# Three of four rounds convolved along the free dimension by VectorE and GpSimd, the fourth by TensorE

## The chip, the cores and the metric

The kernel runs on one core of a Trainium2 chip. The core has TensorE (matrix products into PSUM), VectorE, ScalarE, GpSimd and SyncE; each runs its own instruction stream in order, and they wait for each other through semaphores. DMA transfers are issued from the queues of SyncE, ScalarE and GpSimd. The metric is the device time of one execution in microseconds (us). A profile of one execution gives, for every instruction, its start, its duration and what it waited for. In profiles PE is TensorE's matmul, PEld its weight load, DVE is VectorE, ACT ScalarE, POOL GpSimd and SP SyncE; L381 is line 381 of the kernel.

## The reference, cut to what matters

```python
# x: (8, 3904, 192) float32, weight: (8 heads, 7 taps)
w = softmax(weight, axis=-1)
x_pad = zeros of 6 tokens ahead of each of the 8 sequences, then x
for each head h (24 channels) and token s:
    conv[b, s, h, :] = sum over k of w[h, k] * x_pad[b, s + k, h, :]
y = conv.reshape(31232, 192)
a = y @ w1; b = y @ w2            # 192 x 1024 each
out = ((a * b) @ w3) @ w_out      # 1024 x 1024, 1024 x 192
```

The convolution is causal: a token's value is a weighted sum of that token and the six before it, with one set of seven weights for each head, and it does not look across the start of a sequence.

## The kernel before, in words

The 31232 tokens are two streams of 15616 tokens (`NS = 2`, `TS`), four sequences each, worked side by side: stream 0 lives in partitions 0 to 63 of a tile and stream 1 in partitions 64 to 127. A *round* is 512 tokens of both streams (`CH`), so there are 31 rounds, the last of half size. Rounds are taken in *groups* of four (`GROUP`); a group first does all its first products and then all its second products.

*First product* (`first_product`, `first_factor` at L381): for each of eight column blocks of 128, TensorE multiplies the transposed tokens `xT` by w1 and by w2, each into a pair of PSUM banks; ScalarE casts the first pair to bf16 (`asb`, L389) and VectorE multiplies it by the second pair into `abT` (L400). *Second product* (`second_product`, L434): w3 and w_out are multiplied once at the start into `W_sb`, so that a round and stream needs only `abT` times `W_sb`: 32 matmuls into one pair of banks, copied by ScalarE to an `osb` buffer (L439) and sent out by one DMA. There are five `osb` buffers (the tag `slot`), and a copy waits until the DMA that read its buffer before is done. `W_sb`'s source `w3T` is a constant tile of the kernel before.

PSUM is four pairs of banks. `banks()` takes the first pair of the list `free`, and `drained(p)` puts a pair back at its end. The list is a matter of the program's text and not of time: which pair an instruction gets is fixed when the program is written, and the instruction then waits for the pair's earlier reader.

*Convolution*: x is loaded by GpSimd's DMA queue in windows of 64 tokens that advance by 58 (`load_x`, L119): partition = token in the window, so the seven taps reach across partitions. `conv` (L290) multiplies a window by a 64x64 band matrix that holds a head's seven weights on its diagonals; VectorE or ScalarE moves the result from PSUM to `convo` (L311). `store` writes `convo` to `rows`, a token-by-token copy in DRAM, by SyncE's queue (L334), and `transposes` reads `rows` back into `xT` by DMA transposes (L363), three for a round. `xT` is a ring of four rounds. Blocks of windows are listed in `SIZES`: six small ones in the prologue, then six of 36 windows, one per group, whose heads are convolved after the second, fourth and eighth second product of a group for the group after next. `send` issues the transposes of a round as soon as its rows are stored. The order on each engine is the order of the program's text (`manual_schedule`); nothing reorders it later.

SyncE's queue issues its DMAs in the order of the text as well: the outputs of the second products, the stores of `rows` and the transposes stand in one line, and one that waits holds those behind it. The output DMAs of group 0 go by GpSimd's queue.

Of the kernel before, what the change touches and what calls it, by code (L numbers as in the profile page):

```python
# [8 lines left out]
FP32 = mybir.dt.float32  # L9
BF16 = mybir.dt.bfloat16  # L10
# [6 lines left out]
def kernel(  # L17
# [31 lines left out]
    SIZES = [6, 4, 8, 10, 8, 20] + [36] * 6  # L49
    assert sum(SIZES) == NWIN  # L50
    NB = len(SIZES)
    FIRST = [sum(SIZES[:b]) for b in range(NB)]
    PROLOGUE_BLOCKS = 6
    EARLY = SIZES[0] * ST
    MAXN = max(SIZES) // 2

# [203 lines left out]

    xT = [const.tile([128, RING + Q], BF16, name=f"xT{k}", tag=f"xT{k}") for k in range(NP)]
# [12 lines left out]
    def conv(b, h0, nh, evict=None):  # L274
        n = SIZES[b] // 2
        if h0 == 0:
            convo_of[b] = work.tile([128, n, NP, NS, Q], BF16, tag="convo", bufs=2, name="convo")
# [132 lines left out]
    def first_product(R, between=None, fts=range(JT), behind_conv=False):  # L410
        if R not in abT_of:
            first_tile(R)
        N = width(R)
        step = CH // N
        for ft in fts[::step]:
            first_part(R, list(range(ft, ft + step)), 0, N)
            if behind_conv and ft == step:
                free[1], free[2] = free[2], free[1]
            if between and ft in between:
                between[ft]()  # L420
# [34 lines left out]
    w3T = const.tile([128, JT, DFF], BF16)  # L455
# [105 lines left out]
    load_x(6)  # L561
    first_product(3)
# [5 lines left out]
    def conv_heads(b, heads, last, f=(nc.vector.tensor_copy,), nh=1):  # L568
        for j, h in enumerate(heads[::nh]):
            conv(b, h, nh, (f[j % len(f)],))  # L570
        if heads[-1] == H - 1:
            first = min(need(sent[0]), FIRST[b] + SIZES[b])
            store(b, last=first)
            send(last)
            store(b, first)
            send(last)

    slots = (range(0, 3), range(3, 6), range(6, H))
    zero(5)
    for jt in range(JT):  # L580
        w3_product(jt)

    groups = [list(range(R, min(R + GROUP, NR))) for R in range(0, NR, GROUP)]
    assert groups[-1][-1] == NR - 1
    for p, rounds in enumerate(groups):
        b = PROLOGUE_BLOCKS + p
        order = rounds[-1:] + rounds[:-1] if rounds[-1] == NR - 1 else rounds
        for j, R in enumerate(order if p else ()):
            first_product(R, behind_conv=j == 0 and b <= NB)
            send(R + GROUP)  # L590
            if j < 2 and b < NB:
                P(out=pace, in_=abT_of[R][0:1, JT - 1, 1, 0:2])  # L592
                load_x(b, (j,))
        if b < NB:
            zero(b)
        ahead = rounds[-1] + GROUP
        at = {1: [(b, slots[0], ahead)], 3: [(b, slots[1], ahead)],
              7: [(b, slots[2], ahead, (V, A))]}
        if p == 0:
            at = {0: [(5, range(0, 6), ahead, (V, A), 2)], 1: [(5, range(6, H), ahead, (V,), 2)],  # L600
                  4: at[1], 5: at[3], 7: at[7]}
        for i, (R, r) in enumerate((R, r) for R in rounds for r in range(NS)):
            second_product(R, r, R == NR - 1 and r == 1, nc.sync if p else nc.gpsimd)
            for c in at.get(i, ()) if b < NB else ():
                conv_heads(*c)
    assert sent[0] == NR
# [30 lines left out]
```

## Time and profile before

| what | value |
|---|---|
| time, median of 3 runs | 519.98 us (519.84 to 521.27) |
| profiled execution | 520.47 us, span 518.8 us, granted TensorE clock 1.0 |
| TensorE matmul busy | 512.4 us, 99% of the span |
| VectorE / ScalarE / GpSimd busy | 352.8 / 328.7 / 58.5 us |
| a group's first products (219.04 to 260.59) | 41.55 us |
| a group's second products (195.77 to 219.04) | 23.27 us |

The span is the time from the first to the last instruction of the profiled execution. Busy time is the union of an engine's instructions. The chain of waits follows the last instruction back to what released it, step by step; the share of an engine or a line in it says how much of the span that line itself set. A row of the groups gives the source line, the engine, the operation, the tiles it writes and reads, their sizes and the number of instructions, then busy time and mean duration, then how long the engine had been idle before them and for whom it waited.

### The profile page before, as it was taken

The page shows a single profiled execution, that of the slowest core. Times are in us where ns is not written, and L with a number is a line of the kernel's source. Part 1 is how long each engine was busy: PE and PEld are TensorE (multiplying, and loading weights), DVE is VectorE, ACT ScalarE, POOL GpSimd, SP SyncE. Part 2 cuts the span into 40 slices and gives each one's busy share as a digit, 9 for nine tenths or more (in the row PEclk, how much of TensorE's full clock was granted, in tenths as well). Part 3 has the DMA queues.
Part 4 walks back from the last instruction along what each step waited for, and adds up shares of the span by engine and source line. Part 5 has one row for each costly group of instructions (what it writes and reads, how often), then busy time and mean ns, then how long its engine had stood idle before and what let it go on. Part 6 is the DMA issues. An engine that isn't in the chain of part 4 may idle for free.

```text
span 518.8 us, 13029 instructions
## 1 busy us (share of the span) xinstructions
PE 512.4 (99%) x5576; PEld 338.7 (65%) x5576; DVE 352.8 (68%) x334; ACT 328.7 (63%) x415; POOL 58.5 (11%) x98
## 2 busy tenths in 40 slices
PE   8999999999999999999999999999999999999997
PEld 4455797445884558845588455884558845599567
DVE  6778625999439994399943999439994399921980
ACT  6887634777347773477734777347773477734762
POOL 8501522110001200011000120001200000000000
PEclk9999999999999999999999999999999999999999
DMA  9979997599246992469924699246992465124004
GB/s 117 162 145 133 156 201 202 137 178 119 93 134 134 151 121 92 135 117 142 143 92 136 141 141 122 93 136 147 133 121 93 136 146 96 37 92 153 1 3 152
DMA packets 133576, 64.61 MB, mean 125 GB/s; under 512 B 90460, under 2 KB 132798, under 8 KB 133454
## 3 DMA queue, kind: packets, MB, share of 16 engines
q1 hardware_dynamic: 94476, 44.06, 41.7%
q0 software_dynamic: 38896, 19.62, 29.1%
q8 instruction: 43, 0.70, 0.6%
q14 instruction: 15, 0.12, 0.1%
q10 hardware_dynamic: 146, 0.10, 0.1%
HBM read 33.25 MB, written 36.52 MB: 134 GB/s over the span
## 4 chain that ended last, share of the span: by engine, by line
PE 95%; DMA 2%; ACT 2%; DVE 1%; issue 0%; ACTq 0%; DVEq 0%
PE pairs L381 58%; PE pairs L434 31%; PE pairs L290 3%; DMA xT<-rows 2%; DVE abT L400 1%; PE pairs L469 1%; ACT asb L389 1%; PE pairs L206 1%; PE pairs L343 1%; PE pairs L256 0%; ACT wd L186 0%; ACT convo L311 0%; DVE convo L478 0%; ACT xT L355 0%; PE pairs L509 0%
## 5 line engine op out<-in xcount | busy, mean ns | idle before, releaser
L400 DVE TENSOR_TENSOR abT<-asb,pairs 128x1024 bf16<-128x1024 bf16 (+1 forms) x245 | 297.9, 1217 | 52.6 <-ACT asb L389 36.6
L381 PE MATMUL pairs<-xT,wd 64*128 64x512 bf16 (+3 forms) x3000 | 319.9, 371 | 1.1 <-DMA xT<-rows 0.5
L389 ACT CAST asb<-pairs 128x1024 bf16<-128x1024 f32 (+1 forms) x245 | 247.2, 1009 | 66.2 <-PE pairs L381 65.9
L381 PEld LDWEIGHTS <-wd 64*128 64x128 bf16 x3000 | 161.0, 94 | 154.8 <-issue 3.7
L434 PEld LDWEIGHTS <-abT 128*128 128x128 bf16 x1952 | 160.0, 98 | 7.5 <-issue 7.5
L434 PE MATMUL pairs<-W_sb,abT 128*128 128x192 bf16 x1952 | 164.9, 246 | 0.0
L439 ACT COPY osb<-pairs 128x384 f32<-128x384 f32 x122 | 58.3, 478 | 113.8 <-PE pairs L434 113.8
L311 DVE CAST convo<-pairs 128x864 bf16<-128x864 f32 (+5 forms) x58 | 46.4, 854 | 95.8 <-PE pairs L290 74.9
L119 POOL DMA_DIRECT2D xb<-in_x_dram x42 | 32.2, 784 | 3.7 <-PE pairs L381 3.7
L592 POOL COPY pace<-abT 1x2 bf16<-1x2 bf16 x10 | 1.8, 176 | 253.5 <-DVE abT L400 253.5
L290 PE MATMUL pairs<-xb,Aband 64*64 64x432 bf16 (+5 forms) x384 | 16.7, 284 | 0.1
L311 ACT CAST convo<-pairs 128x864 bf16<-128x864 f32 (+4 forms) x20 | 11.8, 626 | 0.4
L290 PEld LDWEIGHTS <-Aband 64*64 64x64 bf16 x384 | 6.9, 106 | 6.8 <-issue 5.7
L446 POOL DMA_DIRECT2D out_dram<-osb x8 | 6.1, 761 | 16.7 <-ACT osb L439 14.1
L439 DVE COPY osb<-pairs 128x192 f32<-128x192 f32 x1 | 0.4, 358 | 11.1 <-PE pairs L434 11.1
L469 PEld LDWEIGHTS <-w3T 128*128 128x128 bf16 x64 | 5.2, 98 | 0.4 <-issue 0.4
L469 PE MATMUL pairs<-wo_b,w3T 128*128 128x192 bf16 x64 | 5.5, 246 | 0.0
L190 POOL COPY wd<-wd 64x768 bf16<-64x768 bf16 x6 | 4.8, 840 | 0.4 <-DMA wd<-in_moe_w_dram 0.4
L206 PE MATMUL pairs<-zeros 128*128 128x512 bf16 x8 | 3.8, 627 | 1.1 <-DVE ones L152 1.1
L343 PE MATMUL pairs<-ident,convo 128*128 128x128 bf16 x48 | 3.9, 219 | 0.7 <-DVE convo L478 0.6
L343 PEld LDWEIGHTS <-convo 128*128 128x128 bf16 x48 | 2.9, 97 | 2.5 <-issue 1.5
L471 ACT CAST W_sb<-pairs 128x192 bf16<-128x192 f32 x8 | 2.6, 320 | 2.8 <-PE pairs L469 2.8
(52 smaller groups left out, 38.8 us busy)
## 6 DMA issues: line engine op xcount, KB each, us to landing
out_dram<-osb SPq DMA_DIRECT2D x52, 384.0 KB
xb<-in_x_dram POOLq DMA_DIRECT2D x16, 432.0 KB, 11.6
rows<-convo SPq DMA_DIRECT2D x5, 648.0 KB
out_dram<-osb POOLq DMA_DIRECT2D x8, 384.0 KB, 3.9
w3rows<-in_moe_w_dram POOLq DMA_DIRECT2D x2, 1024.0 KB, 11.5
xb<-in_x_dram POOLq DMA_DIRECT2D x8, 240.0 KB, 5.5
xT<-rows SPq DMA_TRANSPOSE x81
rows<-convo SPq DMA_DIRECT2D x3, 432.0 KB
```

The costliest lines, as they stand in the source:

```text
L119: nc.gpsimd.dma_start(out=xb[Q * r:Q * r + Q, w:w + m, :], in_=x_spans(r, i, m))
L206: nc.tensor.matmul(t[:, j % 2, :], zeros, zeros[:, 0:1].to_broadcast([128, CH]), start=True, stop=True)
L290: nc.tensor.matmul(view(slice(Q * c, Q * c + Q), r)[:, :, j * G:(j + 1) * G], band_of(h, r), xb[Q * r:Q * r + Q, w0:w0 + n, h * G:(h + 1) ...
L311: f[e % len(f)](out=dst, in_=part)
L343: nc.tensor.transpose(out=tps[:, w, :], in_=convo[:, w, k].rearrange("p r g -> p (r g)"), identity=ident)
L381: nc.tensor.matmul(p[:, r, e * n:e * n + n], wd[i][rs, k, ft * 128:(ft + 1) * 128], xT[k][rs, r0 + c0:r0 + c1], start=(k == 0), stop=(k == ...
L389: nc.scalar.copy(out=asb, in_=pa)
L400: nc.vector.tensor_tensor(out=dst, in0=asb, in1=pb, op=ALU.mult)
L434: nc.tensor.matmul(ops[:, (g - g0) * D:(g - g0) * D + D], ab[:, jt, r, g * 128:(g + 1) * 128], W_sb[:, jt, :], start=(jt == 0), stop=(jt = ...
L439: f(out=osb[:, g0:g0 + per, :].rearrange("p g d -> p (g d)"), in_=ops[:, 0:per * D])
L446: queue.dma_start(out=out[t0:t0 + ng * 128, :].rearrange("(g p) d -> p g d", p=128), in_=osb)
L469: nc.tensor.matmul(wps[:, 0, 0:D], w3T[:, gt, jt * 128:(jt + 1) * 128], wo_b[:, gt, :], start=(gt == 0), stop=(gt == JT - 1))
```

## The change

The prologue's blocks are now `[6, 4, 8, 10, 8, 20, 20, 14]`, which covers rounds 0 to 9. The rest is split in two kinds. Rounds 10 and 11, 13 to 15, 17 to 19, 21 to 23, 25 to 27, and 29 and 30 are *shares* (`SHARED`, numbered 0 to 5); rounds 12, 16, 20, 24 and 28 are *alone* (`ALONE`).

A round alone is convolved by TensorE with the band matrices as before, in one block of ten windows, right after the first second product of its group: heads 0 to 3 moved by VectorE, heads 4 to 7 by ScalarE.

A share is loaded by `load_shared` with tokens along the free dimension: partition p holds W consecutive tokens (12 for three rounds, 8 for share 0, 6 for share 5) and the six ahead of them, both streams and all 192 channels. Where a sequence starts in a share (shares 1 and 3), a further DMA writes zeros over the six tokens ahead of it, after the loads. The seven taps are then seven shifted views of one partition's row. `shared_head` convolves a head in one of two ways. On VectorE: ScalarE writes tap 6 into a pair of PSUM banks, VectorE adds taps 5 to 1 in place (`scalar_tensor_tensor`) and writes tap 0 plus that sum to `y` in two pieces, or four where a head crosses a multiple of 64 channels. On GpSimd: a multiplication for each tap and an addition for each but the first, in fp32 tiles in SBUF. `store_shared` writes `y` to `rows` with one DMA on SyncE's queue. A share's heads go to GpSimd and VectorE as 5 and 3 (share 0), 6 and 2 (share 1) and 4 and 4 (shares 2 to 5). Share p is worked in group p and stored, from share 1 on, after the second first product of group p + 1; its transposes follow the store on the queue. The softmax of the weights is computed a second time, on all partitions, into `wv`. `w3T` moves into the buffers of the shares' loads. The exchange of two PSUM pairs (`behind_conv`) and the small copies `pace` that held back GpSimd's loads are gone.

```diff
-    SIZES = [6, 4, 8, 10, 8, 20] + [36] * 6
+    SIZES = [6, 4, 8, 10, 8, 20, 20, 14]
+    SHARED = [(2 * GROUP + 2, 3 * GROUP)] + [
+        (R + 1, min(R + GROUP, NR)) for R in range(3 * GROUP, NR, GROUP)]
+    ALONE = {p: (p + 2) * GROUP for p in range(1, len(SHARED))}
+    NA = 2 * (-(-CH // (2 * ST)))
+    SIZES += [NA] * len(ALONE)
...
+    def load_shared(v):
+        t0, W = share(v)
+        xv = work.tile([128, W + PAD, NS, D], BF16, tag="xw", bufs=2, name="xv")
+        for r in range(NS):
+            nc.gpsimd.dma_start(out=xv[:, :, r, :], in_=bass.AP(
+                tensor=x.tensor, offset=(r * TS + t0 - PAD) * D,
+                ap=[[W * D, 128], [D, W + PAD], [1, D]]))
+        for s0 in range(0, TS, S):
+            if 0 <= s0 - t0 < 128 * W:
...
+                nc.gpsimd.dma_start(
+                    out=pad, in_=zeros[0:1, :].unsqueeze(1).to_broadcast([1, PAD * NS * D // 128, 128]))
...
+    def shared_head(v, h, f):
...
+        if on_vector:
+            p, pair = banks()
+            acc = pair.rearrange("p r c -> p (r c)")[:, 0:W * NS * G]
+        else:
+            acc = work.tile([128, W * NS * G], FP32, tag="acc", bufs=2, name="acc")
...
+        if on_vector:
+            nc.scalar.activation(out=flat, in_=xs(PAD), func=ACT.Copy, scale=tap(PAD))
+            for k in range(PAD - 1, 0, -1):
+                f.scalar_tensor_tensor(out=flat, in0=xs(k), scalar=tap(k), in1=flat,
+                                       op0=ALU.mult, op1=ALU.add)
+            for dst, r, cs in parts:
+                f.scalar_tensor_tensor(
+                    out=dst, in0=xv[:, 0:W, r, h * G + cs.start:h * G + cs.stop],
+                    scalar=tap(0), in1=by_row[:, :, r, cs], op0=ALU.mult, op1=ALU.add)
+            drained(p)
+            return
+        f.tensor_scalar_mul(out=flat, in0=xs(PAD), scalar1=tap(PAD))
+        for k in range(PAD - 1, -1, -1):
+            term = work.tile([128, W * NS * G], FP32, tag="term", bufs=2, name="term")
+            f.tensor_scalar_mul(out=term.rearrange("p (m g) -> p m g", g=G), in0=xs(k),
+                                scalar1=tap(k))
+            if k:
+                f.tensor_tensor(out=acc, in0=acc, in1=term, op=ALU.add)
+        term = term.rearrange("p (s r g) -> p s r g", r=NS, g=G)
+        for dst, r, cs in parts:
+            f.tensor_tensor(out=dst, in0=by_row[:, :, r, cs], in1=term[:, :, r, cs], op=ALU.add)
...
+    mine = {1: {0: (0, 5), 1: (0, 6), 2: (0, 7), 3: (1, 6), 4: (1, 7)}}
+    for v in range(2, len(SHARED)):
+        mine[v] = {0: (v, 4), 1: (v, 5), 3: (v, 6), 4: (v, 7)}
...
     for p, rounds in enumerate(groups):
-        b = PROLOGUE_BLOCKS + p
         order = rounds[-1:] + rounds[:-1] if rounds[-1] == NR - 1 else rounds
         for j, R in enumerate(order if p else ()):
-            first_product(R, behind_conv=j == 0 and b <= NB)
-            send(R + GROUP)
-            if j < 2 and b < NB:
-                P(out=pace, in_=abT_of[R][0:1, JT - 1, 1, 0:2])
-                load_x(b, (j,))
...
+            first_product(R)
+            if j == 1 and p - 1 in ALONE:
+                store_shared(p - 1)
+            if R + GROUP < NR and (p > 1 or j < 2):
+                transposes(R + GROUP)
+            if j == 1 and p > 1 and p in ALONE:
+                pool_heads(p, range(0, 4), lambda: load_next(p + 1))
         for i, (R, r) in enumerate((R, r) for R in rounds for r in range(NS)):
             second_product(R, r, R == NR - 1 and r == 1, nc.sync if p else nc.gpsimd)
...
+            elif p in ALONE:
+                if i == 0:
+                    for h, f in ((0, V), (GROUP, A)):
+                        conv(PROLOGUE + p, h, GROUP, (f,))
+                    store_alone(p)
+                if i in mine[p]:
+                    shared_head(*mine[p][i], nc.vector)
+            if p == 1 and i == 4:
+                pool_heads(1, range(0, 6), lambda: load_next(2))
+        if p == 0:
+            load_next(1)
+            pool_heads(0, range(0, 5))
+        if p == 1:
+            store_shared(0)
+            for R in range(*SHARED[0]):
+                transposes(R)
```

`pool_heads` calls `shared_head` on GpSimd for the heads listed and calls `load_next` after the second of them; `load_next(v)` issues the loads of round alone v and of share v.

More of the change, by code (lines that the diff above doesn't have):

```diff
@@ L261, with store_shared @@
+    def store_shared(v):
+        t0, W = share(v)
+        y = shared.pop(v)[1]
+        nc.sync.dma_start(
+            out=rows[t0:t0 + 128 * W, :].rearrange("(p s) c -> p (s c)", s=W),
+            in_=y.rearrange("p s k r q -> p (s k r q)"))
     xT = [const.tile([128, RING + Q], BF16, name=f"xT{k}", tag=f"xT{k}") for k in range(NP)]
@@ L276, in conv @@
         if h0 == 0:
-            convo_of[b] = work.tile([128, n, NP, NS, Q], BF16, tag="convo", bufs=2, name="convo")
+            tag, bufs = ("convo", 2) if b <= PROLOGUE else ("alone", 1)
+            convo_of[b] = work.tile([128, n, NP, NS, Q], BF16, tag=tag, bufs=bufs, name="convo")
         convo = convo_of[b]
@@ L561 @@
     load_x(6)
+    wv = const.tile([128, H, K], FP32)
+    top = const.tile([128, H], FP32)
+    nc.sync.dma_start(out=wv, in_=bass.AP(
+        tensor=weight.tensor, offset=0, ap=[[0, 128], [K, H], [1, K]]))
     first_product(3)
```

112 lines of the change are left out of this document (86 added, 26 removed).

## The prediction

> **What bounds the kernel now.** I read the page's busy times and its chain first, then the table of stages, then the groups of instructions kept apart by shape, and last GpSimd and the DMA queue of SyncE in order of time.
>
> ```profile
> span 518.8 us, 13029 instructions
> PE 512.4 (99%) x5576; PEld 338.7 (65%) x5576; DVE 352.8 (68%) x334; ACT 328.7 (63%) x415; POOL 58.5 (11%) x98
> PE 95%; DMA 2%; ACT 2%; DVE 1%; issue 0%; ACTq 0%; DVEq 0%
> PE pairs L381 58%; PE pairs L434 31%; PE pairs L290 3%; DMA xT<-rows 2%; DVE abT L400 1%; PE pairs L469 1%; ACT asb L389 1%; PE pairs L206 1%; PE pairs L343 1%; PE pairs L256 0%; ACT wd L186 0%; ACT convo L311 0%; DVE convo L478 0%; ACT xT L355 0%; PE pairs L509 0%
> ```
>
> TensorE is the bound: 99% busy and 95% of the chain. Convolution (L290) is only 3% of the chain, so moving it away can give little; GpSimd is idle for 89%. The table of stages shows what the two kinds of stage leave free (stretch, length, then PE, PEld, DVE, ACT, POOL busy, clock, DMA share):
>
> ```profile
> 88.78:130.95 42.17, 41.72 (x385) 20.86 (x386) 38.43 (x32) 32.79 (x34) 4.55 (x7) 1.00 0.93 140
> 195.77:219.04 23.27, 23.27 (x290) 21.63 (x292) 7.74 (x11) 8.05 (x17) 0.00 (x0) 1.00 0.36 120
> 219.04:260.59 41.55, 41.55 (x386) 20.66 (x386) 38.42 (x32) 32.79 (x34) 3.74 (x6) 1.00 1.06 129
> 455.05:476.28 21.23, 21.23 (x259) 21.07 (x260) 1.59 (x2) 7.59 (x16) 0.00 (x0) 1.00 0.40 131
> ```
>
> A group of four rounds is 41.55 us of first products and 23.27 us of second products, 64.8 us. In the first products VectorE has 38.4 of 41.5 us to do; its room is the 15.5 us idle in the second products. A stage of second products without convolution takes 21.23 us, so 2.0 us of a group is all that could go. The groups by shape give the prices (busy us, mean ns):
>
> ```profile
> L400 DVE TENSOR_TENSOR abT<-asb,pairs 128x1024 bf16<-128x1024 bf16 x242 | 295.3, 1221 | 51.6 <-ACT asb L389 35.6
> L439 ACT COPY osb<-pairs 128x384 f32<-128x384 f32 x121 | 58.0, 479 | 112.9 <-PE pairs L434 112.9
> L290 PE MATMUL pairs<-xb,Aband 64*64 64x432 bf16 x192 | 12.3, 352 | 0.0
> L290 PE MATMUL pairs<-xb,Aband 64*64 64x120 bf16 x32 | 0.8, 219 | 0.0
> L311 DVE CAST convo<-pairs 128x576 bf16<-128x576 f32 x12 | 9.0, 747 | 0.0
> L311 DVE CAST convo<-pairs 128x288 bf16<-128x288 f32 x12 | 5.4, 447 | 0.0
> L311 DVE CAST convo<-pairs 128x640 bf16<-128x640 f32 x1 | 0.8, 815 | 0.0
> L311 DVE CAST convo<-pairs 128x320 bf16<-128x320 f32 x1 | 0.5, 481 | 0.0
> L311 ACT CAST convo<-pairs 128x640 bf16<-128x640 f32 x3 | 2.1, 696 | 0.0
> L311 ACT CAST convo<-pairs 128x320 bf16<-128x320 f32 x3 | 1.3, 428 | 0.1
> L190 POOL COPY wd<-wd 64x768 bf16<-64x768 bf16 x6 | 4.8, 840 | 0.4 <-DMA wd<-in_moe_w_dram 0.4
> L592 POOL COPY pace<-abT 1x2 bf16<-1x2 bf16 x10 | 1.8, 176 | 253.5 <-DVE abT L400 253.5
> ```
>
> **What TensorE saves.** Groups 1 to 5 lose a block of 36 windows each (32 matmuls of 432 columns) and get the lone round's 32 matmuls of 120 columns: 0.8 us. The chain prices the old block:
>
> ```profile
> 201.16 0.67 PE pairs L290 x12
> 207.21 0.67 PE pairs L290 x12
> 218.55 0.49 PE pairs L290 x8
> 219.04 41.55 PE pairs L381 x384
> ```
>
> 0.67 + 0.67 + 0.49 = 1.83 us, so 1.03 us a group and 5.1 us in all, 1.0%. Group 0 swaps 36 windows for 20 + 14: nothing. The one-time weight preparation is six operations on 128x56 elements or fewer, beside TensorE's first product 3 and first `w3_product`: under 1 us, and I count it at nothing.
>
> **VectorE's heads.** A head of three rounds is 576 elements per partition: ScalarE writes tap 6 into a pair of PSUM banks, VectorE adds five taps in place and then writes tap 0 in two pieces of 288 (heads 2 and 5 in four). No row has this operation. A cast of 576 takes 747 ns, of 288 447 ns (300 ns for 288 elements); by that slope 1024 elements would take 1214, and the two-input multiplication takes 1221, so a second input costs nothing and the cast rows price it: 5 x 0.747 + 2 x 0.447 = 4.63 us, head 5 (two of 192, two of 96: 0.347, 0.247) 4.92. From below nothing goes under 5 x 0.60 + 0.60 = 3.6 us, the slope alone.
>
> TensorE has no part in a head, but the head keeps its PSUM pair until its last piece, and pairs are handed out in a list fixed by the program. With four pairs a, b, c, d, a full group reads: second product 0 a, lone convolution b and c, head d; product 1 a, head b; product 2 c; product 3 d, head a; product 4 b, head c; products 5, 6, 7 d, a, b. So product 3 waits for the first head, product 4 for the second, product 6 for the third. In us from the stage's start, 2.67 a product: products 0 to 2 and the 0.8 of convolution end at 8.8. ScalarE casts the lone round's second half (0.696 + 0.428 from 3.5) and writes tap 6 (about 0.65): the first head starts at 5.3 and ends at 9.9, the others at 14.85, 19.5 and 24.1. Product 3 runs 9.95 to 12.6, product 4 from 14.9, 5 to 20.2, 6 to 22.9, 7 to 25.55. The stage takes 25.6 us, not 23.27: +2.3. The same reckoning gives +2.6 for group 1 (three heads of 384 elements, two of 576, product 6 waiting for the fourth), +2.3 for groups 2, 3 and 4, and -1.0 for group 5 (288 elements, no wait). Sum: **+8.5 us**; TensorE's saving is in it.
>
> What else moves is covered: ScalarE's tap 6 is four times 0.65 us in a stage where it has 8 of 23 us to do, and its casts for the old block (one of 864 elements a group) go. Loads stay four DMAs a group and the stores of `rows` become six instead of up to seven, at a DMA share of 0.36 in that stage; the reads grow by the six rows that each partition's run repeats (18 rows for 12), beside first products whose transposes are what TensorE needs next, half a stage later. If that cover is gone, the transposes are late, which the next part prices.
>
> **GpSimd's heads and the queue behind them.** A head on GpSimd is seven multiplications and five additions of 576 elements and one more in two pieces. The copies of 768 elements (840 ns) and 2 (176 ns) give 0.866 ns per element over about 175 ns: a multiplication of 576 is 0.67 us. An addition reads two fp32 tiles; no row of GpSimd has two inputs. Ends: the copy's rate, and three times it. I take twice, one pass per input, as nearest to the row that exists: 1.17 us. A head is then 7 x 0.67 + 5 x 1.17 + 2 x 0.67 = 11.9 us (ends 8.9 and 14.9); of 384 elements 8.8 (6.8, 10.8); two pieces more cost 0.35. The Trainium skill, GPSIMD Engine Reference, section 3.1, says that GpSimd's two inputs share one port, with 4497 ns for an addition of 2048 fp32 elements; by that 576 would take about 1.26 us, a head 12.3 and the sum below would be some 4 us more; no run so far shows it.
>
> Four heads and four DMAs are about 52 us in a group of 67: steady groups hold. The start does not:
>
> ```profile
> 89.09 0.75 POOL L446 DMA_DIRECT2D out_dram<-osb  x1 [1.89 <-ACT osb L439]
> 101.57 1.74 POOL L119 DMA_DIRECT2D xb<-in_x_dram  x2 [0.36 <-PE pairs L381]
> xb<-in_x_dram POOLq DMA_DIRECT2D x16, 432.0 KB, 11.6
> out_dram<-osb POOLq DMA_DIRECT2D x8, 384.0 KB, 3.9
> ```
>
> GpSimd is free of group 0's output at 89.8; four loads take 3.5 (0.87 each). Share 1 holds a sequence start (token 7808), so a DMA of zeros waits until the loads land: 11.6 us for 432 KB; these are 864 KB each, and I take 15 (between 11.6 and 23). Then 0.9, five heads of share 0 (44.2) and six of share 1 (72.3) with four loads between (3.5): GpSimd ends share 1 at P = **229 us** (201 and 257 at the ends).
>
> SyncE's queue puts that share's store behind first product 9 of group 2, at about 178, and nine transposes and all outputs of group 2 behind the store:
>
> ```profile
> 199.06 20.41 SPq L446 DMA_DIRECT2D out_dram<-osb  x8
> 223.30 4.99 SPq L363 DMA_TRANSPOSE xT<-rows  x3
> 233.86 19.78 SPq L363 DMA_TRANSPOSE xT<-rows  x9
> ```
>
> Five `osb` buffers let five second products end; ScalarE's copy of the sixth waits for the first output. That lands at P + 0.5 + 6 (the store; estimate, between the 3.9 and 11.6 above) + 15 (nine transposes at 4.99 / 3, with other DMA idle) + 3.9, P + 25. Three more products' copies, the last two behind further outputs, then first product 12 goes on as if begun at P + 29 = 258. Before it began at 219.0; unhindered but for VectorE it would at 224. From there 299.8 us of the old span remain, and 2 x 2.3 - 1.0 more: 258 + 303.4 = 561.6 to 562, and 1.7 us stand outside the span (520.47 against 518.8; the median of the runs, 519.98, is 0.5 below the profiled run). Share 2 is 4 heads, loads and another wait for zeros: 67.5 us after P, and its store would be late by 0.4 us; afterwards GpSimd gains on TensorE. Sum: **564 us**.
>
> **Rivals.** (1) GpSimd is in time; only VectorE's heads hold PSUM: 520.5 + 8.5 = 529 us. It needs P at or under about 195, six less than at the copy's rate: with the zeros' wait hidden and additions as cheap as copies it comes out. For it: GpSimd's idle 89%. (2) Faster: no pair is waited for and P is in time: 520.5 - 5.1 = 515.4. It decides if the first head is done by 8.8, so takes 3.5 us, below the slope alone; or if ScalarE and VectorE begin sooner than I set them. (3) The two cancel: 520. (4) GpSimd is the bound throughout: above 15.9 us a head, four heads with 3.5 us of DMA exceed 67 us. At 17 us P is 277, and shares 2 and 3 are late too: about 637. Against it: three times the copy's rate is still under 15.9. A shared port could bring it: the Trainium skill, SBUF — State Buffer, section Who interferes with whom, lets VectorE and GpSimd block each other when VectorE reads two inputs from SBUF. Here line L400 reads `asb` from SBUF and `pairs` from PSUM, and so do the new heads, so by that rule GpSimd is left alone and case 4 stays small.
>
> **How the numbers follow.** GpSimd late at the start: 0.61, between 535 (the copy's rate) and 604 (three times, share 2 late by 12). Rival 1: 0.24; rival 2: 0.06; rival 3: 0.03; rival 4: 0.06. The time is the likeliest case's, 564. The range 526 to 602 leaves out rivals 2, 3, 4 and a little of each end. A difference of 0.3% is about what these runs can tell from none: faster 0.06, same 0.03, slower 0.91.
>
> **What would show it.** In the changed kernel's profile: matmuls of the convolution fall by about 10 us; VectorE's taps of 576 near 0.75 us; second products 3 and 4 waiting for VectorE in groups 2 to 4 and stages of 25.6 us; GpSimd's additions near 1.2 us; SyncE's store of share 1 waiting for GpSimd until about 229, and TensorE idle from about 224 to 256. Wrong would be: GpSimd's additions at 0.7 us or 1.7, its last head of share 1 before 195, or a wait for outputs that ends well before the ninth transpose.

## The result, and the profile after

The changed kernel takes 748.33 us (median of 4 runs, 746.49 to 750.04), the kernel before 519.91 us beside it: 1.438 times as long, 95% interval 1.434 to 1.443. The forecast was 564 us with a range from 526 to 602. The direction was right; the size was not, by 184 us. The profiled execution took 746.49 us with a span of 744.8.

First the page of the changed kernel: busy times, four of the rows in 40 slices, and the chain that ended last by engine and by line.

```profile
span 744.8 us, 13655 instructions
...
PE 537.5 (72%) x5608; PEld 382.8 (51%) x5608; DVE 417.4 (56%) x459; ACT 341.5 (46%) x446; POOL 551.0 (74%) x477
...
PE   8999898969349354000799722997649992899998
...
POOL 9124320999999999999956999999999999960000
...
PEclk9999999989769588555699975999959997799999
...
POOL 29%; PE 14%; DMA 3%; issue 2%; SPq 1%; ACT 0%; POOLq 0%; ACTq 0%
POOL term L326 14%; POOL acc L329 9%; PE pairs L485 9%; PE pairs L536 5%; POOL acc L323 2%; POOL y L332 2%; SPq L467 1%; DMA xv<-in_x_dram 1%; DMA out_dram<-osb 1%; POOL xv L279 1%; DMA rows<-y 1%; POOL xb L338 0%; ACT osb L541 0%; POOL xv L288 0%; ACTq L541 0%
```

The bound has moved. Before, TensorE was busy in every slice and was 95% of the chain. Now GpSimd (the row POOL) is full from slice 8 to slice 35, but for slices 21 and 22, where it stands for 12.9 us ahead of share 3's zeros, and it leads the chain; TensorE stands idle for whole slices, and its clock falls with it. GpSimd's multiplications (L326) are the chain's largest line, its additions (L329) stand beside TensorE's first product (L485).

Next the groups of instructions of the changed kernel, kept apart by shape (busy us, mean ns | idle before them), first GpSimd's, then VectorE's:

```profile
L326 POOL TENSOR_SCALAR term<-xv,wv 128x576 f32<-128x576 bf16 x108 | 186.3, 1725 | 0.0
L329 POOL TENSOR_TENSOR acc<-acc,term 128x576 f32<-128x576 f32 x90 | 126.0, 1400 | 7.5
L326 POOL TENSOR_SCALAR term<-xv,wv 128x384 f32<-128x384 bf16 x30 | 37.3, 1244 | 0.0
...
L332 POOL TENSOR_TENSOR y<-acc,term 128x288 bf16<-128x288 f32 x26 | 20.0, 791 | 1.1
L288 POOL DMA_DIRECT2D xv<-zeros x2 | 1.1, 565 | 37.0 <-DMA xv<-in_x_dram 24.1 <-issue 12.9
...
L315 DVE SCALAR_TENSOR_TENSOR pairs<-xv,wv,pairs 128x576 f32<-128x576 bf16 x70 | 57.6, 822 | 12.2 <-ACT pairs L313 10.2
L318 DVE SCALAR_TENSOR_TENSOR y<-xv,wv,pairs 128x288 bf16<-128x288 bf16 x22 | 10.3, 512 | 0.6
```

A GpSimd head of 576 elements is 7 x 1.725 + 5 x 1.400 + 2 x 0.791 = 20.7 us, not 11.9 (21.0 from the start of one to the start of the next). Four of them and their DMAs are about 88 us; a group of four rounds took 64.8 us before. A VectorE head is 5 x 0.822 + 2 x 0.512 = 5.1 us, against 4.63.

The waits of the changed kernel (us in total, times, longest) show how GpSimd's lateness reaches TensorE:

```profile
ACT osb L541 <- DMA out_dram<-osb: 167.3, 12, 76.4
PE pairs L485 <- ACT osb L541: 133.6, 8, 69.4
PE pairs L536 <- DVE y L318: 23.3, 8, 7.3
```

The longest one in order of time, SyncE's queue and then TensorE (start, us, what):

```profile
337.72 0.36 SPq L360 DMA_DIRECT2D rows<-y  x1
341.94 11.55 SPq L467 DMA_TRANSPOSE xT<-rows  x9
353.58 0.53 SPq L548 DMA_DIRECT2D out_dram<-osb  x1
```

```profile
357.23 1.81 PE L485 MATMUL pairs<-xT,wd 64*128 64x512 bf16 x6 [69.39 <-ACT osb L541]
```

Share 1's last head ends at 337. Its store leaves at 337.7, the nine transposes at 341.9 to 353.5, the first output only behind them, and TensorE, whose results sit in full `osb` buffers, goes on at 357.2 after 69.4 us. The same happens to shares 2, 3 and 4, with waits of 26.0, 15.2 and 16.4 us.

### The profile page after: what moved, and what is told of

It reads as the page before. It is cut to its first block, busy times and chain, and to the rows that moved or that the text cites. A ratio compares the mean times of both kernels' runs of the same rounds, so it can differ in the third digit from the quotient of the medians.

```text
span 744.8 us, 13655 instructions
## 1 busy us (share of the span) xinstructions
PE 537.5 (72%) x5608; PEld 382.8 (51%) x5608; DVE 417.4 (56%) x459; ACT 341.5 (46%) x446; POOL 551.0 (74%) x477
## 5 line engine op out<-in xcount | busy, mean ns | idle before, releaser
L485 PE MATMUL pairs<-xT,wd 64*128 64x512 bf16 (+3 forms) x3000 | 341.2, 384 | 161.9 <-ACT osb L541 133.6
L485 PEld LDWEIGHTS <-wd 64*128 64x128 bf16 x3000 | 197.2, 96 | 299.6 <-issue 168.2
L326 POOL TENSOR_SCALAR term<-xv,wv 128x576 f32<-128x576 bf16 (+2 forms) x162 | 247.7, 1529 | 0.0
L536 PEld LDWEIGHTS <-abT 128*128 128x128 bf16 x1952 | 167.6, 101 | 29.7 <-issue 28.2
L329 POOL TENSOR_TENSOR acc<-acc,term 128x576 f32<-128x576 f32 (+2 forms) x135 | 166.8, 1235 | 11.3
L315 DVE SCALAR_TENSOR_TENSOR pairs<-xv,wv,pairs 128x576 f32<-128x576 bf16 (+2 forms) x105 | 77.4, 737 | 14.6 <-ACT pairs L313 11.5
L323 POOL TENSOR_SCALAR acc<-xv,wv 128x576 f32<-128x576 bf16 (+2 forms) x27 | 41.4, 1535 | 0.1
L332 POOL TENSOR_TENSOR y<-acc,term 128x288 bf16<-128x288 f32 (+6 forms) x68 | 39.1, 601 | 2.3
L415 DVE CAST convo<-pairs 128x640 bf16<-128x640 f32 (+5 forms) x21 | 14.7, 743 | 43.4 <-PE pairs L394 36.2
L288 POOL DMA_DIRECT2D xv<-zeros x2 | 1.1, 565 | 37.0 <-DMA xv<-in_x_dram 24.1
L394 PE MATMUL pairs<-xb,Aband 64*64 64x120 bf16 (+5 forms) x416 | 10.8, 228 | 16.4 <-DMA xb<-in_x_dram 16.4
L548 POOL DMA_DIRECT2D out_dram<-osb x8 | 6.2, 774 | 20.7 <-ACT osb L541 18.7
L318 DVE SCALAR_TENSOR_TENSOR y<-xv,wv,pairs 128x288 bf16<-128x288 bf16 (+6 forms) x52 | 19.2, 419 | 1.0
L394 PEld LDWEIGHTS <-Aband 64*64 64x64 bf16 x416 | 7.2, 110 | 21.5 <-DMA xb<-in_x_dram 12.8
L126 POOL DMA_DIRECT2D xb<-in_x_dram x22 | 15.4, 720 | 2.2 <-DMA xb<-in_x_dram 1.8
## 6 DMA issues: line engine op xcount, KB each, us to landing
out_dram<-osb POOLq DMA_DIRECT2D x8, 384.0 KB, 13.3
```

Source lines behind the costliest of these rows:

```text
L315: f.scalar_tensor_tensor(out=flat, in0=xs(k), scalar=tap(k), in1=flat, op0=ALU.mult, op1=ALU.add)
L323: f.tensor_scalar_mul(out=flat, in0=xs(PAD), scalar1=tap(PAD))
L326: f.tensor_scalar_mul(out=term.rearrange("p (m g) -> p m g", g=G), in0=xs(k), scalar1=tap(k))
L329: f.tensor_tensor(out=acc, in0=acc, in1=term, op=ALU.add)
L332: f.tensor_tensor(out=dst, in0=by_row[:, :, r, cs], in1=term[:, :, r, cs], op=ALU.add)
L415: f[e % len(f)](out=dst, in_=part)
```

## The experiments

**probe: what makes GpSimd's multiplication slow.** In the kernel `light` (next but one), four rounds of eleven single operations on 576 elements were added behind two of the shares. The run (551.78 us, a single one) serves for the prices alone.

```
+            f.tensor_scalar_mul(out=term3, in0=rows3, scalar1=tap)      # L709
+            f.tensor_scalar_mul(out=term, in0=flat, scalar1=tap)        # L710
+            f.tensor_scalar_mul(out=acc3, in0=rows3, scalar1=0.5)       # L711
...
+            f.tensor_copy(out=term3, in_=rows3)                         # L713
...
+            f.tensor_scalar_mul(out=half16, in0=flat, scalar1=tap)      # L716
+            f.tensor_tensor(out=term3, in0=rows3, in1=tap broadcast, op=ALU.mult)   # L717
+            f.tensor_tensor(out=acc, in0=acc, in1=term, op=ALU.add)     # L718
```

> GpSimd's heads are cut to one multiplication by tap 6 per piece of y (six taps left out), and after shares 2 and 3 GpSimd runs eleven forms of 576 elements, four times each. The changed kernel's multiplication takes 1.725 us for 576 elements (2.5 ns per element over 0.28), where a copy at 0.866 ns per element would take 0.67. Theory strides: the rows of 24 out of 192 channels cost it; then the contiguous form with the same scalar takes about 0.7 and the strided copy about 1.7. Theory scalar: the multiplication by a scalar per partition costs it; then strided and contiguous take 1.7 alike and the constant 0.5 or the copy take 0.7. Theory conversion: bf16 to fp32 costs it; then the contiguous copy to fp32 takes 1.7 too and fp32 to fp32 takes 0.7.

The groups by shape of this run (busy us, mean ns):

```profile
L716 POOL TENSOR_SCALAR term<-xv,wv 128x576 bf16<-128x576 bf16 x8 | 13.8, 1722 | 0.0
L710 POOL TENSOR_SCALAR term<-xv,wv 128x576 f32<-128x576 bf16 x8 | 13.8, 1722 | 0.8
L709 POOL TENSOR_SCALAR term<-xv,wv 128x576 f32<-128x576 bf16 x8 | 13.8, 1719 | 0.0
...
L711 POOL TENSOR_SCALAR acc<-xv 128x576 f32<-128x576 bf16 x8 | 13.2, 1648 | 0.0
L718 POOL TENSOR_TENSOR acc<-acc,term 128x576 f32<-128x576 f32 x8 | 11.2, 1399 | 0.6
L717 POOL TENSOR_TENSOR term<-xv,wv 128x576 f32<-128x576 bf16 x8 | 9.2, 1146 | 0.0
...
L713 POOL CAST term<-xv 128x576 f32<-128x576 bf16 x8 | 5.3, 664 | 0.0
```

Neither the strides of the rows (L709 against L710), nor the conversion to fp32 (L716), nor the scalar read from memory (L711, a constant) makes the price: all lie between 1.65 and 1.72 us. A plain copy of the same elements costs 0.66 us, which is what the prediction took for a multiplication (0.67). The multiplication by a scalar is a dearer operation on this engine, dearer even than the multiplication of two tensors (1.15); why is not shown.

**pool_ttb: the cheaper multiplication in the full work.**

```
-        f.tensor_scalar_mul(out=flat, in0=xs(PAD), scalar1=tap(PAD))
+        f.tensor_tensor(out=flat, in0=xs(PAD), in1=<tap PAD broadcast over 576>, op=ALU.mult)
...
-            f.tensor_scalar_mul(out=term..., in0=xs(k), scalar1=tap(k))
+            f.tensor_tensor(out=term..., in0=xs(k), in1=<tap k broadcast>, op=ALU.mult)
```

> The changed kernel with one operation exchanged and nothing left out: on GpSimd the multiplication of a tap is a TENSOR_TENSOR with the weight broadcast (1.15 us for 576 elements in the probe) in place of TENSOR_SCALAR (1.72). Theory the operation's price on GpSimd is the step that was mis-sized: a head falls from 21.0 to 17.0 us, share 4 ends 18 x 4.0 + 5 x 2.8 = 86 us earlier, and the time falls to about 662. Theory the place or the number of instructions matters more than the price: above 720.

It took 658.36 us (two runs; about 662 expected), ratio 1.263 (1.253 to 1.273), 90 us less than the changed kernel, with this row for the multiplication:

```profile
L326 POOL TENSOR_TENSOR term<-xv,wv 128x576 f32<-128x576 bf16 x108 | 123.8, 1147 | 0.0
```

A head falls by 7 x 0.578 = 4.0 us, so one us of a head's time is worth about 22 us of the kernel. That is nearly one for one: up to the end of share 4 GpSimd works 18 heads of 576 elements and five of 384, about 21.5 heads in all. That GpSimd is the bound, and what its multiplication's price costs, is shown by this run.

**light, light_all, light_apart: the change without GpSimd's time.** In `light` each GpSimd head keeps only the multiplication by tap 6; everything else stays (heads on VectorE, loads, stores, waits).

```
         f = nc.gpsimd
-        (seven multiplications, five additions, the two pieces)
+        for dst, r, cs in parts:
+            f.tensor_scalar_mul(out=dst, in0=xv[:, PAD:PAD + W, r, ...], scalar1=tap(PAD))
```

> GpSimd's heads are cut to one multiplication by tap 6 per piece of y (six taps left out), all else stays. If GpSimd's throughput alone made the changed kernel slow, the time falls from 748 to what VectorE's heads cost: stages of second products of 26.5 us in groups 2 to 4 as in the changed kernel's profile (505.7 to 532.2), so 520.5 + 3 x 3.2 + 3 - 1 = 532 us, 527 to 537. If those heads hide once everything is in time: 515. If the queue behind SyncE's store or the loads were the cause: above 560.

It took 546.87 us, ratio 1.052 (1.049 to 1.056), above the 527 to 537 expected. So about 201 of the 228 us that the change costs go with GpSimd's heads. The remaining 27 are still above what the prediction had for VectorE (8.5). The first stage of second products in table form (stretch, length, busy PE, PEld, DVE, ACT, POOL, clock, DMA share), then two stretches of 5 us around its longest wait, then the second stage and the fourth; and the wait of TensorE for VectorE:

```profile
137.47:167.18 29.71, 24.07 (x292) 23.18 (x290) 24.44 (x41) 11.33 (x23) 17.24 (x21) 0.89 0.88 158
158.00:163.00 5.00, 3.22 (x21) 2.96 (x21) 4.86 (x7) 0.42 (x1) 5.00 (x7) 0.50 1.30 194
163.00:168.00 5.00, 5.00 (x53) 4.34 (x53) 1.80 (x4) 1.50 (x4) 3.63 (x6) 0.90 1.60 193
208.72:236.87 28.15, 23.86 (x290) 22.88 (x290) 23.16 (x34) 11.22 (x22) 4.22 (x5) 0.94 0.65 144
347.83:374.32 26.49, 22.20 (x291) 21.50 (x290) 23.07 (x34) 11.21 (x22) 0.00 (x0) 1.00 0.45 134
```

```profile
PE pairs L530 <- DVE y L318: 19.2, 8, 5.6
```

The five stages take 29.7, 28.2, 27.9, 26.5 and 22.7 us, 134.9 in all against 5 x 23.27 = 116.4 before: +18.6, where the prediction had +8.5. (Another 7.2 us are group 0, which ends at 96.0 us instead of 88.8.) The second row shows a part that it had left out: around the longest wait, of 5.6 us, the granted clock is 0.50, and it is back to 0.90 only in the next 5 us. The Trainium skill, TensorE: Matmul & The Clock Gate, Part 1, says the array falls to half rate after an idle window of about 3.4 us and needs about as long to come back; these two rows agree. Shorter waits can do it too: in the second and in the fourth stage TensorE waits the same two times, 1.7 and 2.6 us, and the clock of the one is 0.94, of the other 1.00; what decides between them isn't shown. Times their clocks (0.89, 0.94, 0.94 and 1.00) the first four stages are 26.2 to 26.5 us, so of their 112 us about 6.6 are the lower clock (an estimate from these figures).

`light_all` moves the heads of VectorE to GpSimd's reduced form as well, so no engine does the heads' arithmetic.

```
-                    shared_head(*mine[p][i], nc.vector)
+                    shared_head(*mine[p][i], nc.gpsimd)
```

> As light, and VectorE's heads are given to GpSimd in the same cut form, so that no head stands on VectorE or in PSUM. What is left is TensorE's saving, forecast at 1.03 us a group in five groups: 515.4 us. If the loads, the stores or the transposes of the new layout cost time of their own: 520 or more.

It took 524.44 us, ratio 1.007 (1.003 to 1.010), not the 515.4 of TensorE's saving alone. One group, from the start of its second products to the start of the next group's:

```profile
137.23:200.65 63.42, 63.42 (x674) 41.95 (x673) 40.30 (x35) 41.11 (x51) 33.79 (x42) 1.00 1.09 186
```

63.4 us a group with TensorE never idle, against 64.8: TensorE's saving is there, 1.4 us a group and 7 in all (the prediction had 5.1). Yet the kernel is no faster, because group 0, which the prediction entered with nothing, ends 6.8 us later (95.6 us; before 88.8). The profile is of the fastest of ten runs (520.86 us); what the slower ones lose besides isn't seen in it. The difference between the medians of `light` and `light_all`, 22.4 us, is the price of VectorE's heads, with ScalarE's writing of tap 6 in it.

`light_apart` is `light` with the heads' PSUM pairs taken out of the second products' way, so that no product waits for a head.

```
-            p, pair = banks()
+            p = free.pop(2)
+            pair = pairs[:, NS * p:NS * p + NS, :]
```

(and the product before gives its pair back ahead of the last two in the list)

> As light, and the PSUM pairs are kept apart in groups 1 to 5: VectorE's heads take two of the four pairs in turn, second products the other two. Theory pairs: the waits of second products for VectorE go, stages take 22.1 us, and the time is 516. Theory VectorE's time: the heads still end 26 us after the stage began, so the next first product's multiplication comes some 2 us late in groups 2 to 5: 522 to 524.

541.42 us, ratio 1.040 (1.036 to 1.043): only 5.5 us came back, so neither of the two forecasts (516; 522 to 524) holds. The wait of this run that stands in their place, and the first products of a group behind such a wait:

```profile
PE pairs L480 <- DVE y L319: 9.8, 4, 3.5
```

```profile
230.02:275.55 45.53, 43.41 (x385) 23.07 (x385) 41.39 (x37) 32.43 (x33) 12.29 (x14) 0.96 0.67 112
```

The waits before second products are gone, and the first products that follow wait instead, 2.1 to 3.5 us in each of four groups, for the last head; with the lower clock behind the wait (0.96 in the row) they take 45.5 to 46.7 us instead of 41.55. Holding a PSUM pair is the form in which the wait shows. VectorE has 23 us of work in a stage (the rows of `light`), about the stage's own length, and that work stays.

**no_zeros, one_less, out_act: the three steps between GpSimd and TensorE.** `no_zeros` leaves out the DMA of zeros into the rows before a sequence start; `one_less` gives one head less of each share to GpSimd and one more to VectorE; `out_act` issues the outputs from ScalarE's queue, so that they don't stand behind the share's store.

```
-                nc.gpsimd.dma_start(out=pad, in_=zeros...)          # no_zeros
...
-        mine[v] = {0: (v, 4), 1: (v, 5), 3: (v, 6), 4: (v, 7)}      # one_less
+        mine[v] = {0: (v, 3), 1: (v, 4), 2: (v, 5), 3: (v, 6), 4: (v, 7)}
...
-                pool_heads(p, range(0, 4), ...)
+                pool_heads(p, range(0, 3), ...)
...
-            second_product(..., nc.sync if p else nc.gpsimd)        # out_act
+            second_product(..., nc.scalar if p else nc.gpsimd)
```

> The changed kernel without the DMAs of zeros at a sequence's start (two tokens' neighbourhoods in shares 1 and 3 are left wrong). In the changed kernel GpSimd waited 24.1 and 12.9 us for the loads ahead of them. Theory GpSimd is the bound from 131 to 615: the time falls by 37 us, to about 711. Theory the wait is covered (GpSimd would wait for the loads anyway at the next head): by less than 10.

> One head of each share from 1 on moves from GpSimd to VectorE (5 and 3 in share 1, 3 and 5 in shares 2 to 5), all taps kept. Theory GpSimd is the bound: each of shares 1 to 4 ends 21.0 us earlier, so 84 less: about 664. Theory VectorE's heads and their PSUM pairs are as much of it: five heads of 5.2 us make the stage some 5 us longer in four groups, and no more than 60 is gained.

> The outputs of groups 1 to 7 are issued from ScalarE's queue, so that no output stands behind a share's store. Theory the queue made the wait: TensorE's 69, 26, 15 and 16 us of waiting for output buffers go and come back nowhere, and the time falls by 100 or more. Theory GpSimd is the bound and the queue is only the place where it is felt: TensorE then waits for the transposes of the share instead, GpSimd still ends share 4 at about 615, and what follows starts some 15 to 25 us earlier at the end: 723 to 735.

Each has two runs. `no_zeros` took 708.31 us: 40 less, about the two waits of GpSimd (24.1 + 12.9 us in the row of L288). What GpSimd waits for is added to the end nearly one for one. `one_less` took 671.69: 76.6 less, although VectorE has a head more in each stage.

`out_act` took 754.73, 6 more, where a gain of some 15 to 25 us or a larger one had been expected. Its waits say where the time is:

```profile
ACT convo L415 <- DMA xT<-rows: 161.9, 4, 89.5
PE pairs L536 <- ACT convo L415: 155.1, 4, 87.7
```

The end of the longest one in order of time, on SyncE's queue (SPq) and on ScalarE and its queue (ACTq), and then VectorE's half of the lone round's copy:

```profile
343.06 11.93 SPq L467 DMA_TRANSPOSE xT<-rows  x9
```

```profile
346.94 0.41 ACTq L548 DMA_DIRECT2D out_dram<-osb  x1
347.52 1.02 ACT L415 CAST convo<-pairs 128x320 bf16<-128x320 f32 x2 [89.45 <-DMA xT<-rows]
```

```profile
L415 DVE CAST convo<-pairs x2: 480/652/824, 257.9 to 258.7; 128x640 bf16<-128x640 f32 x1, 128x320 bf16<-128x320 f32 x1
```

ScalarE now issues the outputs itself. The first output of this group's second products leaves only at 346.9 us, 3.9 us after the first of the share's transposes (3.9 to 4.0 in the three groups after it), and the lone round's copy, next in ScalarE's stream, follows it; TensorE waits for that copy. The buffer `convo` was free: VectorE wrote its half of it at 257.9. So the outputs weren't freed from the share; the wait changed its name and kept its length. Why an output's issue is held there isn't shown, and this run can't part its two theories. That GpSimd's time is what makes the share late is shown by `pool_ttb`, `one_less`, `no_zeros` and `light`.

**light_early, light_paced: where group 0's 6.8 us go.** Both start from `light_all`. `light_early` loads block 7 together with block 6 and has seven `xb` buffers. `light_paced` also holds the loads of share 0 and of the next lone round and share back until the second first product of group 1 is done.

```
+    load_x(7)                      # light_early: ahead of first product 3
...
-                    load_x(7)
...
-                if i == 3:             # light_paced
-                    load_shared(0)
...
+            if p == 1 and j == 1:
+                P(out=pace, in_=abT_of[R][0:1, JT - 1, 1, 0:2])
+                load_alone(1)
+                load_shared(0)
+                pool_heads(0, range(0, 5))
+                load_shared(1)
```

> As light_all (all heads cut to tap 6 on GpSimd, the other taps left out), with block 7's windows loaded right behind block 6's (seven buffers xb in place of five). In light_all groups 1 to 5 took 63.4 us each where before they took 64.8, but group 0 ended 6.8 us later, TensorE waiting for block 7's loads. Theory those loads are all of it: the 6.8 us go, and the time is 513 to 516. Theory group 0 is late for another reason (DMA traffic of the shares' loads): 519 or more.

> As light_early (all eight heads of each share reduced to the multiplication by tap 6 and done on GpSimd, so work is left out), but the loads of share 0 and of the lone round of group 1 are issued only when the second first product of group 1 is done, not during group 0. If the time that group 0 and the start of group 1 lost in light_early (the waits for the transposes at 88.7 to 93.3 us) came from the traffic of the shares' loads, about 6 us come back: 513 to 517. If it came from something else (the 20 and 14 windows in the place of 36, the order of the stores) the time stays at 519 to 523. If the lone round's loads now land too late for group 1's second stage, the wait for xb stands in the profile there and the time is 518 or more with group 0 repaired.

`light_early` took 521.14 us, ratio 1.000 (0.998 to 1.003). The wait for `xb` is gone and another stands at the start of group 1:

```profile
PE pairs L479 <- DMA xT<-rows: 4.2, 3, 2.4
```

`light_paced` took 525.58 us, ratio 1.009 (1.006 to 1.013), above the 513 to 517 forecast for a mended group 0; the wait for `xb` that its third theory named isn't there either (0.2 us). The stretch that it was to mend is whole; this is TensorE from 85 to 140 us, first in `light_early`, then in `light_paced`:

```profile
85.00:140.00 55.00, 50.81 (x474) 28.49 (x472) 40.75 (x35) 35.03 (x38) 19.39 (x28) 0.94 1.10 161
```

```profile
85.00:140.00 55.00, 55.00 (x589) 33.25 (x587) 41.99 (x37) 38.48 (x46) 15.69 (x21) 1.00 0.91 137
```

But the loads now fall where the next share's loads and the outputs are, and TensorE waits there:

```profile
PE pairs L479 <- ACT osb L535: 4.5, 2, 4.3
PE pairs L479 <- DMA xT<-rows: 2.4, 3, 1.2
```

From 180 to 225 us of this run (size, median us from issue to landing):

```profile
xv<-in_x_dram POOLq DMA_DIRECT2D x2, 864.0 KB, 19.8
xT<-rows SPq DMA_TRANSPOSE x12, 8.8
```

The transposes take 8.8 us there, while two loads of 864 KB are under way; their median over the whole of this run is 4.1, and 2.6 in the changed kernel. So what eats the 7 us that TensorE saves goes with the shares' loads, and moving them in time moves the wait. That their traffic delays the transposes and the outputs is the likeliest reading; no run takes the traffic alone away. The Trainium skill, DMA: Bandwidth & Descriptors, section Issuing engines are not separate DMA queues, says that transfers issued by different engines run on the same 16 DMA engines and interleave; the rows agree, with loads from GpSimd's queue and transposes from SyncE's.

**two_of_four, two_of_four_b: the idea in a smaller size.** Two rounds of four are shared from group 2 on, with multiplications of two tensors; five of the eight heads on GpSimd, three on VectorE (384 elements each), and a share is stored a group later than it is computed. In the second one the zeros are sent between two heads of the share before, the last share is stored in the middle of group 6, and half of the lone rounds' convolution stands at the stage's end.

```
+    SHARED = {v: ((v + 2) * GROUP + 2, min((v + 3) * GROUP, NR)) for v in range(1, 6)}
...
+            if j == 1:
+                load_next(v + 1)
+            if j == 3 and v + 1 in SHARED:      # two_of_four_b
+                zero_shared(v + 1)
...
+            if p == 6 and i == 3:               # two_of_four_b
+                store_shared(5)
+                transposes(SHARED[5][0])
```

> All of the reference's work. Groups 0 and 1 as in the kernel before (TensorE convolves rounds 0 to 13); then two rounds of four are a share (14, 15, 18, 19, 22, 23, 26, 27, 30) of 384 elements a head, five heads on GpSimd with multiplication as TENSOR_TENSOR and three on VectorE, the first share all on GpSimd; two rounds of four stay with TensorE; a share is stored at the end of the next group. By rows: GpSimd's head 7 x 0.8 + 5 x 1.0 + 1.14 = 11.7 us, five and four DMAs 62 us of a group's 64; VectorE's head 3.9 us, three in a stage. If both fit, groups 2 to 5 save 0.7 us each: 517. If the margins are too thin (GpSimd late for a group's end, or pairs waited for): 525 to 545.

> Complete work. As two_of_four, with three orders changed: the zeros of the next share are sent after the fourth head of the share before, not after its last; the share of the last group is stored in the middle of group 6's second stage; and the lone rounds' second half of heads is convolved at the end of the stage. GpSimd needs about 65.5 us for its five heads and its loads in each group, the groups about 64. If the waits of two_of_four (25.6 us for the zeros in group 2, 8 to 13 us for the late last share) were all of its loss: 518 to 525. If GpSimd's 65.5 us are late by themselves, the wait for the share's rows grows from group to group and the time is 525 to 540. Faster than the kernel before, under 518, only if the TensorE time saved by two rounds in four (some 0.7 us a group and more with no wait) is not lost in the stage's waits for VectorE.

560.54 us, ratio 1.076 (1.070 to 1.082), above both of its forecasts, and 534.83 us, ratio 1.026 (1.024 to 1.029), in the range that has GpSimd late. The longest wait that is left in the second one, and the stretch where it lies:

```profile
PE pairs L542 <- DVE y L322: 11.8, 1, 11.8
```

```profile
274.00:287.00 13.00, 1.25 (x15) 1.08 (x14) 4.43 (x10) 1.13 (x3) 12.13 (x16) 0.64 0.17 56
```

VectorE's head waits there for the zeros that GpSimd sends at 280.6, right behind the head before them: GpSimd is busy for 65 of each 70 us from 140 to 420 us in this run and has no room to catch up. Neither version beats the kernel before. Of the versions that do the complete work the best is 2.6% slower.

## Why the prediction was right or wrong

The step that failed is one term of the sum: a multiplication on GpSimd, priced at 0.67 us from rows of plain copies. It takes 1.72 us. The prediction gave the addition two ends and the multiplication none, of GpSimd's operations its signs of being wrong name only the additions, and rival 4 ("GpSimd is the bound throughout", 0.06) was put aside because three times the copy's rate for the additions stays under 15.9 us a head. With the multiplication at its real price even the cheapest addition passes that point: 7 x 1.725 alone is 12.1 us, and 5 x 0.67 + 2 x 0.42 more is over 16. Rival 4 is what happened, at 21 us a head instead of the 17 for which it gave 637; `pool_ttb`, whose heads take 17 us, took 658. Two estimates say what the one term is worth. By the 22 us of kernel time for each us of a head that `pool_ttb` shows, a multiplication of 0.67 us would have given about 748 - 22 x 7 x 1.055 = 586 us; but that slope was measured between 21 and 17 us a head, and at 13.3 us GpSimd would no longer be full in each group. By the prediction's own chain, with share 1 done 70 us earlier (the point on P below), it would have been 564 + 38 = 602, or a little more where share 2 is late too. So the term is some 140 to 160 of the 184 us of the miss.

Point by point:

- *TensorE saves 5.1 us*: the mechanism holds, with 1.4 us a group and 7 in all (`light_all`). Convolution matmuls are 10.8 us busy in the changed kernel, against 16.7: they fell by 5.9, not by the 10 named as a sign, which is about what the five old blocks alone would give, without the lone rounds' new ones (160 of 230 ns, 3.7 us).
- *Group 0: nothing*: wrong by 6.8 us in `light_all`, where TensorE waits for block 7's loads; in `light_early`, without that wait, it waits for transposes instead.
- *VectorE's heads, +8.5*: the size was low. Taps of 576 take 0.822 us (0.747 taken). Products 3 and 4 do wait for the heads, and in the changed kernel the stage from 505.7 to 532.2 takes 26.5 us at full clock (the row below) against 25.6 forecast. With TensorE on time (`light`) the five stages cost +18.6 instead of +8.5: of the 10 us more about 6.6 are the lower clock, which the prediction left out, and the rest fits the heads' size (5.1 us for 4.63, two heads ahead of product 4). Without TensorE's saving the prediction's price is 8.5 + 5.1 = 13.6, to be set against the 22.4 between `light` and `light_all`.

```profile
505.73:532.22 26.49, 22.19 (x289) 21.50 (x289) 23.07 (x34) 8.81 (x17) 25.91 (x20) 1.00 0.11 46
```

- *PSUM pairs as the cause*: right in a small part. With the pairs apart 5.5 of the 22.4 us come back; the rest goes with VectorE's time.
- *Additions on GpSimd, 1.17 us*: 1.40. The estimate of 1.26 from the figure in the Trainium skill, GPSIMD Engine Reference, section 3.1, was nearer but still low. The measured price does not depend on VectorE: the multiplication takes 1.724 us at 300 to 335 us, where VectorE is idle, and 1.726 at 505 to 532, where it is busy for 23 of 26 us (the row above; below, the first stretch, then count and least, median and largest ns of the multiplication in the two). The rule of the Trainium skill, SBUF — State Buffer, section Who interferes with whom, by which GpSimd is left alone here, agrees with these rows; it was no defence against a slow instruction.

```profile
300.00:335.00 35.00, 0.00 (x0) 0.00 (x0) 0.00 (x0) 0.00 (x0) 34.16 (x24) 0.50 0.00 0
```

```profile
L326 POOL TENSOR_SCALAR term<-xv,wv x11: 1724/1724/1725, 300.4 to 334.1; 128x576 f32<-128x576 bf16 x11
...
L326 POOL TENSOR_SCALAR term<-xv,wv x7: 1722/1726/1727, 508.0 to 529.0; 128x576 f32<-128x576 bf16 x7
```

- *P, the end of share 1's last head*: 337 instead of 229. Of the 108 us, 22 lie before the first head: the zeros leave at 130.6 us, after a wait of 24.1 (15 taken) and another of 8.1 for the loads. The other 86 are the eleven heads, 70 of them the multiplications (42 x 1.055 + 35 x 0.736).
- *The queue behind it*: right in its order: store, nine transposes in 11.6 us (15 taken), output, copy, TensorE. TensorE goes on at P + 20; the prediction had the first output landing at P + 25 and TensorE going on as if begun at P + 29.
- *Afterwards GpSimd gains on TensorE*: wrong, for the same reason. With 88 us of work in a group of about 67, it falls behind in every group.

## What to carry to other kernels

Price each operation by a row of the same operation on the same engine; a copy's row bounds arithmetic from below only, and where no row exists the upper end must be tried against the point at which the engine becomes the bound. Give an idle engine work only up to its time per stage, waits for its own DMAs included, for once it is late its time comes back at the end nearly one for one, and a us more in each head as often as there are heads, through buffers and queues that look unrelated. What is gained by removing work from the bounding engine can be lost to the traffic and the waits that the replacement brings: here 7 us saved on TensorE came to nothing even when the replacement's arithmetic was almost free.

## What of the hardware had not been expected

- On GpSimd a multiplication by a scalar costs 1.72 us for 576 elements (1.65 with a constant), against 1.15 for a multiplication of two tensors with the weight broadcast, 1.40 for an fp32 addition and 0.66 for a copy. From 1.244 us at 384 elements the slope is (1.725 - 1.244) / 192 = 2.5 ns per element, nearly three times the copy's 0.87.
- After the 69-us wait TensorE runs at half its clock for the first 9 us, in which it waits once more for 1.7 us; these are the changed kernel's stretches from 357 to 372 us:

```profile
357.00:361.00 4.00, 2.10 (x7) 0.54 (x7) 0.00 (x0) 1.38 (x4) 3.92 (x5) 0.50 0.84 262
361.00:366.00 5.00, 5.00 (x25) 2.07 (x25) 2.35 (x2) 3.61 (x6) 4.83 (x4) 0.50 0.99 317
366.00:372.00 6.00, 6.00 (x57) 3.65 (x55) 4.99 (x5) 4.19 (x5) 5.83 (x5) 0.99 0.17 59
```

  A wait of 5.6 us (`light`) is enough for it, and two of 1.7 and 2.6 us were in some stages and not in others. So a wait that recurs in each stage can cost more than its length.
